# An mLSTM layer with an MLP on one core: one of two large constant products at the start replaced by 80 small ones

## The chip, the cores and the metric

The kernel runs on one core of a Trainium2 chip. Its time is the device time of one execution in microseconds (us). Of the kernel before there are three timed runs, 430.77 us in the median (430.69 to 431.53), and one execution with the hardware profiler on.

## The reference, cut to what matters

The first half is a recurrence over 768 time steps with a 40x40 state for each of 4 batches and 8 heads (mLSTM); the second half is a two-layer MLP on its output.

```python
for t in range(S):                                       # B, H, S, D = 4, 8, 768, 40
    m_new = np.maximum(f_gate[:, :, t] + m, i_gate[:, :, t])
    f_stab = np.exp(f_gate[:, :, t] + m - m_new); i_stab = np.exp(i_gate[:, :, t] - m_new); m = m_new
    C = f_stab * C + i_stab * outer(v_t, k_t)            # 40x40 per batch and head
    n = f_stab * n + i_stab * k_t
    y_t = sigmoid(o_gate_t) * (C @ q_t) / max(|n @ q_t|, 1)
x = y.transpose(0, 2, 1, 3).reshape(3072, 320)
h = x @ w_in                                             # 320 -> 2048
return (h * sigmoid(h)) @ w_out                          # 2048 -> 320
```

Nothing of the reference is touched by the change: the products that it replaces are of a constant with itself, and what they write is never read.

## The kernel before, in words

The 768 time steps are cut into chunks of 64 (`L`), and two batches are taken together, so that there are 24 units (`Unit`). Three units make one step of the MLP (`Step`, eight of them, 384 tokens each), and while step j's MLP runs, the three units of step j+1 are worked into it. The MLP of a step has 16 slices of the 2048 hidden features; of each, `mm1` (L849) makes the hidden values and `mm2` (L901) adds their share of the output. From the second step on each float32 product is split into three of a faster 32-bit kind.

The first three units have nothing to hide behind: they are the head of the program, some 20 us, and they are written out by hand from L987 on. No scheduler moves anything. Each engine runs its instructions in the order in which the code records them, and an instruction waits only for what it reads or overwrites.

The steps of the head that matter here, in the order of TensorE's (PE's) own queue:

- L998 to L1001: `dummy`, a PSUM tile that nobody reads, receives the product of the identity matrix with itself, 128x128 times 128x512 in float32, twice. Each shows as two records of a matmul in the trace. They wait only for `ident`, which GpSimd makes.
- `mask` (L396): for three units a 128x128 by 128x512 product in bfloat16 puts the causal mask into a PSUM tile. It reads `identb` and `maskb`, the bfloat16 copies that ScalarE makes in L117 and L118.
- `scores` (L549): k times q of the first unit, 16 products that show as 32 records. It waits for the DMA of `qk`.
- `small(32)` (L985): 32 more products into `dummy`, 128x128 by 128x64 in bfloat16.
- `expo` (L405, L409): the decay exponents of the first unit. These read `terms`, the gate values split into bfloat16 parts, which VectorE makes in a row of small operations (L167 to L162, called through `gates` and `thirds`) after the two gate tensors have landed.

After that ScalarE takes the exponential (L419), VectorE weighs the scores with it (L576), and so on through three units to the first MLP step at L849.

Of the kernel before, what the change touches and what calls it, by code (L numbers as in the profile page):

```python
# [43 lines left out]
def mlstm_mlp_kernel(  # L44
# [12 lines left out]
    nc = tc.nc  # L57
# [19 lines left out]
    ident = cp.tile([128, 128], F32, name="ident")  # L77
# [9 lines left out]
    identb = cp.tile([128, 128], BF16, name="identb")  # L87
# [76 lines left out]
    def gates(lo, hi):  # L164

        init = NEG if lo == 0 else m_t[:, lo - 1 : lo]
        nc.vector.tensor_tensor_scan(  # L167
            m_t[:, lo:hi], f_t[:, lo:hi], i_t[:, lo:hi], init, op0=ALU.add, op1=ALU.max
        )
        yield  # L170
        l1 = max(lo, 1)
        tt = nc.vector.tensor_tensor
        tt(out=f_t[:, l1:hi], in0=f_t[:, l1:hi], in1=m_t[:, l1 - 1 : hi - 1], op=ALU.add)
        yield
        tt(out=f_t[:, l1:hi], in0=f_t[:, l1:hi], in1=m_t[:, l1:hi], op=ALU.subtract)
        nc.vector.tensor_scalar(f_t[:, l1:hi], f_t[:, l1:hi], -120.0, None, op0=ALU.max)
        if lo == 0:
            nc.vector.memset(f_t[:, 0:1], 0.0)
        yield
        nc.vector.tensor_tensor_scan(  # L180
            LF[:, lo:hi], pat[:, lo:hi], f_t[:, lo:hi], 0.0, op0=ALU.mult, op1=ALU.add
        )
        yield
        tt(out=i_t[:, lo:hi], in0=i_t[:, lo:hi], in1=m_t[:, lo:hi], op=ALU.subtract)
        tt(out=i_t[:, lo:hi], in0=i_t[:, lo:hi], in1=LF[:, lo:hi], op=ALU.subtract)
        yield
# [165 lines left out]
    def wload(n):  # L352
        for p in parts[nload[0] : nload[0] + n]:
            p.load()
        nload[0] = min(nload[0] + n, len(parts))
# [613 lines left out]
    dummy = psO.tile([128, 512], F32, tag="o", name="dummy")  # L969
# [25 lines left out]
    wload(2)  # L995
    u2.load_ko()
    wload(2)
    for _ in range(2):  # L998
        nc.tensor.matmul(  # L999
            dummy, ident, ident.unsqueeze(1).broadcast_to([128, 4, 128]), start=True, stop=True  # L1000
        )  # L1001
    two = gates(2 * L, 4 * L)
    near, far = spread(2 * L, 4 * L, nc.gpsimd), spread_far(4 * L, S, nc.gpsimd)
    late = [gates(4 * L, 8 * L), gates(8 * L, S)]
# [253 lines left out]
```

## Time and profile before

| | us |
|---|---|
| median of three timed runs | 430.77 (430.69 to 431.53) |
| the profiled execution, its whole time | 431.02 |
| its span, first to last instruction | 429.2 |
| PE busy in the span | 422.4 (98%) |
| DVE, ACT, POOL busy | 288.5, 220.6, 124.8 |

PE is TensorE's matmuls and PEld its weight loads, DVE VectorE, ACT ScalarE, POOL GpSimd, SP SyncE, which issues most DMAs. The whole time is 1.82 us longer than the span. A start time in the rows is in us from the start of the span. The profile has a column for the clock that TensorE was granted, as a share of full speed; its record begins only with the first change of the clock, and ahead of that the column reads 1.00. How fast TensorE really went there is read from the pace of its instructions.

### The profile page before, as it was taken

The numbers are of one execution on the slowest core, as the hardware profiler recorded it, in microseconds if no ns is written. First come the engines' busy times: TensorE is split into PE (matmuls) and PEld (weight loads), VectorE is DVE, ScalarE is ACT, GpSimd is POOL, SyncE is SP. The second block draws the span as 40 slices with busy tenths as digits, with TensorE's granted clock in tenths as the row PEclk, the third lists the DMA queues.
The fourth block names the chain that finished last, engine by engine and source line by source line (L and its number), as shares of the span: only waits on it lengthen the run. The fifth ranks groups of instructions, "written<-read, shape, count | busy, mean of one in ns | idle before, by whom it ended". The sixth has DMA issues, their size and how long they took to land.

```text
span 429.2 us, 12518 instructions
## 1 busy us (share of the span) xinstructions
PE 422.4 (98%) x5062; PEld 391.7 (91%) x5062; DVE 288.5 (67%) x650; ACT 220.6 (51%) x481; POOL 124.8 (29%) x135
## 2 busy tenths in 40 slices
PE   8999999999999999999999999999999999999995
PEld 4767677899999999999999999999999999999995
DVE  5888799877887677467765677566764756443342
ACT  7684866755755454454454644444454543353331
POOL 5734135234234423043412344034320400000000
PEclk9999999999999999999999999999999999999999
DMA  8999696334551775127660575316750231001001
GB/s 272 387 366 311 177 299 165 117 89 141 159 169 21 196 196 155 31 61 189 174 172 2 123 218 139 118 25 179 209 163 22 54 94 20 18 9 39 2 2 46
DMA packets 62650, 57.17 MB, mean 133 GB/s; under 512 B 31440, under 2 KB 49184, under 8 KB 62592
## 3 DMA queue, kind: packets, MB, share of 16 engines
q1 hardware_dynamic: 62288, 55.94, 45.7%
q8 instruction: 40, 0.66, 0.7%
q10 hardware_dynamic: 208, 0.26, 0.2%
q0 software_dynamic: 96, 0.16, 0.1%
q14 instruction: 18, 0.15, 0.1%
HBM read 48.99 MB, written 7.36 MB: 131 GB/s over the span
## 4 chain that ended last, share of the span: by engine, by line
PE 80%; issue 17%; DVE 1%; ACT 1%; POOL 0%; POOLq 0%; ACTq 0%; DVEq 0%
PE ph L849 35%; PE pout L901 33%; PE p L549 3%; PE p L637 2%; PE p L620 2%; PE dummy L999 1%; PE pu_u L705 1%; PE pu_h L705 1%; DVE D L576 0%; PE e L396 0%; PE px L794 0%; PE pu L717 0%; PE po L604 0%; PE p L794 0%; POOL qt L533 0%
## 5 line engine op out<-in xcount | busy, mean ns | idle before, releaser
L856 ACT ACTIVATE th<-ph 128x384 f32<-128x384 f32 x128 | 62.4, 488 | 106.7 <-PE ph L849 106.2
L849 PE MATMUL ph<-xh,wh 128*128 128x384 f32 x336 | 113.8, 339 | 0.0
L849 PE MATMUL ph<-xl,wh 128*128 128x384 f32 x336 | 113.6, 338 | 0.0
L901 PE MATMUL pout<-woh,gh 128*128 128x320 f32 x336 | 105.5, 314 | 0.0
L901 PE MATMUL pout<-woh,gl 128*128 128x320 f32 x336 | 103.9, 309 | 0.0
L901 PE MATMUL pout<-wol,gh 128*128 128x320 f32 x336 | 103.3, 307 | 0.0
L876 ACT CAST gh<-th 128x384 fp32r<-128x384 f32 x112 | 57.5, 513 | 81.3 <-DVE th L871 69.9
L880 DVE TENSOR_TENSOR gl<-th,gh 128x384 fp32r<-128x384 f32 x112 | 64.6, 577 | 47.5 <-ACT gh L876 47.5
L871 DVE SCALAR_TENSOR_TENSOR th<-th,ph 128x384 f32<-128x384 f32 x112 | 61.4, 548 | 51.1 <-ACT th L856 50.6
L849 PE MATMUL ph<-xh,wl 128*128 128x384 f32 x224 | 75.9, 339 | 0.0
L747 POOL TENSOR_TENSOR Cm<-Cm,lq 40x328 f32<-40x328 f32 x40 | 30.6, 764 | 114.6 <-PE p L637 111.8
L901 PEld LDWEIGHTS pout<-woh,gh 128*128 128x128 f32 x336 | 63.0, 188 | 0.9
L849 PEld LDWEIGHTS ph<-xh,wh 128*128 128x128 f32 x336 | 63.1, 188 | 0.2
L849 PEld LDWEIGHTS ph<-xl,wh 128*128 128x128 f32 x336 | 63.0, 188 | 0.2
L901 PEld LDWEIGHTS pout<-woh,gl 128*128 128x128 f32 x336 | 63.0, 188 | 0.1
L901 PEld LDWEIGHTS pout<-wol,gh 128*128 128x128 f32 x336 | 63.1, 188 | 0.0
L533 POOL TENSOR_TENSOR qt<-qk,lq 104x512 f32<-104x512 f32 x22 | 29.7, 1348 | 99.4 <-ACT lq L529 89.3
L849 PEld LDWEIGHTS ph<-xh,wl 128*128 128x128 f32 x224 | 42.1, 188 | 0.0
L901 PE MATMUL pout<-wo,g 128*128 128x320 f32 x96 | 28.7, 435 | 0.0
L516 POOL TENSOR_TENSOR D<-D,am 128x512 f32<-128x512 f32 x20 | 26.1, 1303 | 4.0 <-DMA D<-LFd 2.5
L508 POOL TENSOR_TENSOR am<-mask,aT 128x512 f32<-128x512 f32 x20 | 24.1, 1205 | 6.6 <-DVE aT L207 5.1
L576 DVE TENSOR_TENSOR D<-p,D 128x512 f32<-128x512 f32 x24 | 16.5, 689 | 13.7 <-PE p L637 12.3
(136 smaller groups left out, 524.4 us busy)
## 6 DMA issues: line engine op xcount, KB each, us to landing
qk<-in_qk_dram SPq DMA_DIRECT2D x24, 512.0 KB, 5.1
ko<-in_ko_dram SPq DMA_DIRECT2D x24, 320.0 KB, 5.3
wro<-in_w_out_dram SPq DMA_DIRECT2D x8, 640.0 KB, 7.3
D<-LFd SPq DMA_DIRECT2D x40, 128.0 KB, 3.1
lq<-LFd SPq DMA_DIRECT2D x40, 128.0 KB, 4.9
wri<-in_w_in_dram SPq DMA_DIRECT2D x8, 512.0 KB, 6.0
vb<-in_vp_dram SPq DMA_DIRECT2D x48, 82.0 KB, 5.1
out_dram<-ob SPq DMA_DIRECT2D x45, 80.0 KB, 2.1
```

The lines of the kernel that those rows point to most:

```text
L508: nc.gpsimd.tensor_tensor(out=self.am, in0=mask.unsqueeze(1).broadcast_to([128, H, L]), in1=aT[:, self.c, self.p, :].unsqueeze(2).broadcas ...
L516: nc.gpsimd.tensor_tensor(out=self.Dm, in0=self.Dm, in1=self.am, op=ALU.add)
L533: nc.gpsimd.tensor_tensor(out=self.qt, in0=self.q[:KS], in1=self.lq[:KS], op=ALU.mult)
L549: nc.tensor.matmul(self.ps[d * L : (d + 1) * L, a * 4 + j, :], self.k[r, d * 4 + j, :], self.q[r, d * 4 + j, :], start=True, stop=True,)
L576: nc.vector.tensor_tensor(out=self.Dm, in0=self.ps, in1=self.Dm, op=ALU.mult)
L747: nc.gpsimd.tensor_tensor(out=v, in0=v, in1=self.lq[r, :, L - 1].unsqueeze(2).broadcast_to([D, H, D1]), op=ALU.mult,)
L849: nc.tensor.matmul(ph, w, x, start=(i == 0), stop=(i == len(ops) - 1))
L856: nc.scalar.activation(th, ph, AF.Tanh, scale=0.5)
L871: nc.vector.scalar_tensor_tensor(out=th, in0=th, scalar=1.0, in1=ph, op0=ALU.add, op1=ALU.mult)
L876: nc.scalar.copy(gh, th)
L880: nc.vector.tensor_tensor(out=gl, in0=th, in1=gh.bitcast(F32), op=ALU.subtract)
L901: nc.tensor.matmul(self.po[t], g[:, ts], w, start=(fc == 0 and i == 0), stop=(last and i == len(ops) - 1),)
```

## The change: what it does

The second of the two large float32 products is gone. In its place stand 80 products in bfloat16 with a contraction of 128, 32 columns of the constant `identb` as weights and 16 columns of it streamed past, into the corner `dummy[:32, :16]` of the same tile. Each has a weight load of its own, so that PE's queue has 160 rows more. Nothing else in the program is touched.

```diff
-    for _ in range(2):
-        nc.tensor.matmul(
-            dummy, ident, ident.unsqueeze(1).broadcast_to([128, 4, 128]), start=True, stop=True
-        )
+    nc.tensor.matmul(
+        dummy, ident, ident.unsqueeze(1).broadcast_to([128, 4, 128]), start=True, stop=True
+    )
+    for _ in range(80):
+        nc.tensor.matmul(dummy[:32, :16], identb[:, :32], identb[:, :16], start=True, stop=True)
```

At the start of PE's queue this stood before (`e_195`, `e_197` and `e_199` are the PSUM tiles of the three units' exponents, and what an instruction waits for stands in brackets):

```order
L999 MATMUL dummy<-ident 128x512 [waits Pool_49]
L999 MATMUL dummy<-ident 128x512
L396 LDWEIGHTS identb [waits Activation_49]
L396 MATMUL e_195<-maskb,identb 128x512 [waits Activation_49]
L396 LDWEIGHTS identb
L396 MATMUL e_197<-maskb,identb 128x512
L396 LDWEIGHTS identb
L396 MATMUL e_199<-maskb,identb 128x512
L549 MATMUL p_201<-qk_152 64x64 [waits DMAHW2_49]
```

And this stands there now; the lines left out are 79 more pairs of the two rows ahead of them:

```order
L998 MATMUL dummy<-ident 128x512 [waits Pool_49]
L1002 LDWEIGHTS identb [waits Activation_49]
L1002 MATMUL dummy<-identb 32x16
...
L396 LDWEIGHTS identb
L396 MATMUL e_274<-maskb,identb 128x512 [waits Activation_49]
L396 LDWEIGHTS identb
L396 MATMUL e_276<-maskb,identb 128x512
L396 LDWEIGHTS identb
L396 MATMUL e_278<-maskb,identb 128x512
L549 MATMUL p_280<-qk_152 64x64 [waits DMAHW2_49]
```

The wait for ScalarE's `identb` has moved from the first mask product to the first of the small products. On every other engine the order is what it was.

Further down PE's queue, at the end of `small(32)`, the rows are the same before and after but for the numbers of the tiles; this is before:

```order
L985 MATMUL dummy<-maskb,identb 128x64
L405 LDWEIGHTS home [waits DVE_49,Activation_49]
L405 MATMUL e_195<-terms,home 128x64 [waits Activation_49]
L405 LDWEIGHTS home
L405 MATMUL e_195<-terms,home 128x64
```

Here PE waits for VectorE and ScalarE, and all that the change adds stands ahead of this wait.

## Rows read from the trace of the kernel before

**Rows 1.** What PE waited for: engine, tile, line; us in total, times, longest.

```profile
PE dummy L999 <- POOL ident masks.py:199: 1.4, 1, 1.4
PE po L604 <- DVE po L655: 0.4, 1, 0.4
PE p L549 <- DVE D L576: 0.2, 1, 0.2
```

**Rows 2.** Three stretches: length, PE busy (instructions), granted clock, DMA.

```profile
14.90:30.00 15.10, 15.10 (x163) 1.00 1.05 390
30.00:100.00 70.00, 69.96 (x784) 1.00 0.68 200
100.00:424.00 324.00, 323.73 (x3887) 1.00 0.38 100
```

**Rows 3.** Chain that ended last, its start: start us, us, what.

```profile
1.36 3.78 PE dummy L999 x4
5.14 1.20 PE e L396 x3
6.34 0.62 PE p L549 x32
6.97 1.04 PE dummy L985 x32
8.01 0.06 issue
8.06 0.39 PE e L405 x8
8.46 0.36 PE e L409 x2
8.81 0.02 issue
8.83 0.60 ACT D L419
```

**Rows 4.** Timeline of PE and PEld: start us, us, instruction, [idle before].

```profile
3.23 0.33 PEld L999 LDWEIGHTS dummy<-ident 128*128 128x128 f32 x1 [0.52 <-issue]
4.08 1.06 PE L999 MATMUL dummy<-ident 128*128 128x512 f32 x1
4.08 0.15 PEld L396 LDWEIGHTS <-identb 128*128 128x128 bf16 x1 [0.52 <-ACT sel L124]
4.93 0.63 PE L396 MATMUL e<-maskb,identb 128*128 128x512 bf16 x1
5.36 0.15 PEld L396 LDWEIGHTS <-identb 128*128 128x128 bf16 x1 [0.28 <-issue]
5.79 0.55 PE L396 MATMUL e<-maskb,identb 128*128 128x512 bf16 x1
6.27 0.69 PE L549 MATMUL p<-qk 40*64 40x64 f32 x32
6.90 1.11 PE L985 MATMUL dummy<-maskb,identb 128*128 128x64 bf16 x32
7.81 0.19 PE L985 MATMUL dummy<-maskb,identb 128*128 128x64 bf16 x1
```

**Rows 5.** Timeline of ACT, DVE and PEld: what PE waits for.

```profile
2.84 0.30 ACT L117 CAST identb<-ident 128x128 bf16<-128x128 f32 x1
7.50 0.40 ACT L161 COPY terms<-middle 32x256 bf16<-32x256 bf16 x1 [0.58 <-DVE middle L160]
7.50 0.42 DVE L162 TENSOR_TENSOR terms<-rest,middle 32x256 bf16<-32x256 f32 x1
8.03 0.16 PEld L405 LDWEIGHTS <-home 96*128 96x128 bf16 x3
```

**Rows 6.** Durations by line: ns min/median/max, first and last start us.

```profile
L396 PE MATMUL e<-maskb,identb x4: 390/592/631, 4.9 to 16.9; 128*128 128x512 bf16 x4
L985 PEld LDWEIGHTS <-identb x32: 95/98/98, 6.9 to 7.8; 128*128 128x128 bf16 x32
L409 PEld LDWEIGHTS <-terms x2: 106/106/106, 8.4 to 8.4; 96*64 96x64 bf16 x2
```

**Rows 7.** Timeline of PE, a later line with small products.

```profile
18.25 0.44 PE L438 MATMUL eq<-terms,sel 96*64 96x64 bf16 x16
```

## The prediction

> **What bounds the kernel now.** I read the waits of TensorE (PE) first, then its busy time by stretches, then the chain of waits from its start, then the timeline of the first 8 us. The waits show that in 429.2 us PE stands idle for only three things: 1.4 us until `ident` is there, then 0.2 and 0.4 us in the head [rows 1]. The stretches show that from 14.9 us on PE is busy all the time: 15.10 of 15.10 us, 69.96 of 70, 323.73 of 324 [rows 2]. So whatever comes later in the head comes off nowhere behind it: a delay of PE at 15 us is a delay of the end, one to one. The reader can see from this that only the first 15 us matter, and there the chain runs through PE: the large products L999, the masks L396, the scores L549, the 32 fillers L985, and then the exponents L405 and L409, ACT's exponential and so on [rows 3].
>
> At one place on this chain another engine is nearly level with PE. L405 reads `terms`; ACT ends its part at 7.90 and DVE at 7.92 (7.50 plus 0.40 and 0.42), and L405's weight load starts at 8.03, 0.11 later [rows 5]. PE had started its last filler at 7.81 [rows 4]. The fillers come every 0.029 us ((7.81 - 6.90) / 31 [rows 4]), so PE could have gone on at 7.84. It had at most 8.03 - 7.84 = 0.19 us to spare; the chain, which puts this place on PE's account until 8.01 [rows 3], says almost none. I take 0.1. A PE that comes earlier than now thus gains nothing, since L405 waits for DVE; a PE that comes later by D costs about D - 0.1.
>
> The second thing to see is the clock. The granted clock reads 1.00 in the stretches [rows 2], but ahead of 6 us the pace tells another level. The masks stream 512 columns each and start at 4.93, 5.36 and 5.79 [rows 4], one in 0.43 us, which is 1.2 columns per ns, the lower level (1.2 GHz). The same line takes 631 ns at most and 390 ns at 16.9 us [rows 6]; the third one, at 5.79, took 0.55 us [rows 4], a third of the way from the slow duration to the fast one. So two thirds of it (0.28 us) passed at the lower level, and the clock rose to 2.4 GHz at about 6.1 us. Up to then PE had worked without a gap since 1.36.
>
> **The change part by part.** Removed are the third and fourth record of L999. The third one's weights load at 3.23, the fourth record starts at 4.08 and the first mask at 4.93 [rows 4], so the two hold PE from 3.23 to 4.93, 1.70 us at the lower clock.
>
> Added are 80 pairs of a weight load and a product. The first load now waits for `identb`, which ACT finishes at 2.84 + 0.30 = 3.14 [rows 5], just ahead of 3.23: this wait costs nothing by itself, but the load, 0.15 us at the lower clock [rows 4], cannot start much ahead of it, so that the first small product starts at about 3.35. Behind it in PE's queue wait the masks, the scores, the fillers and L405; nobody else waits for `dummy`.
>
> What a pair costs is not in this trace, and it decides the result. From above: the fillers, 128 weight columns and 64 streamed ones, take 29 ns at the full clock; if a small pair were no cheaper, it would take 59 ns at the lower one, 80 of them 4.7 us. From below: L438 starts 16 products of 64 columns within 0.44 - 0.20 = 0.24 us [rows 7] (0.20 is about what one filler takes, 0.19 [rows 4]), 16 ns each at the full clock, because two strips of columns work side by side; if pairs came as fast as that whatever the clock, 80 would take 1.3 us. The nearest row is L438 by strip: two products every 32 ns, so 32 ns for a load of 64 columns and a product of 64 columns in one strip. The small pair loads 32 and streams 16, all in one strip; at half the load it would take 16 ns at the full clock and 32 ns at the lower. I take 32 ns: 80 x 32 = 2.56 us, and the small products end at 3.35 + 2.56 = 5.91 where the large one ended at 4.93.
>
> The Trainium skill, "TensorE: Matmul & The Clock Gate", section "LDWEIGHTS (loading the stationary operand)", has a load cost its columns divided by 1.2 per ns. That is 27 ns for 32 columns, an estimate from that page; 80 of them would be 2.1 us, the delay worked out below 0.2 us and the time 431.0. The trace does not bear the rule out in durations (64 columns 106 ns, 128 columns 95 to 98 ns [rows 6]), and no row here has a load of 32 columns.
>
> Now the rest up to L405, with the clock rising at 6.1 as before. The first mask starts at 5.91, does 0.19 / 0.43 = 44% by 6.1 and the rest at 0.21 us per mask, ending at 6.22; the two others at full clock end at 6.64. Before, the third ended at 6.1 plus a third of 0.21, so 6.14, and L549 started 0.13 later at 6.27 [rows 4]; now it starts at 6.77, 0.50 later. The scores and fillers run at the full clock as before, so PE reaches L405 0.50 late and, with 0.1 to spare, L405 starts 0.4 late. The saving on the masks (0.43 to 0.21) gives back half of what the small products cost; without it the delay were 0.98.
>
> Sum: 0.4 us. Nothing behind it absorbs this: ACT's exponential, DVE's weighing and PE's next products follow each other on the chain. The profiled execution took 431.02 with a span of 429.2, so it would be 431.4; it stands 0.25 above the median of the runs, 430.77. Against the median that is 431.2. By the bounds of a pair, the masks would end at 6.0 (no delay, L405 waits for DVE) at 16 ns; at 59 ns, with 47 pairs done at 6.1 and 33 at 29 ns, the small products end at 7.07, the masks at 7.71, L549 starts 1.57 late, and L405 1.5 late: 432.2.
>
> **The rivals.** *PE still arrives before DVE.* If a pair takes 25 ns or less, the small products end by 5.35 and the masks by 6.2, and L405 goes with DVE as now: 430.8. For it speaks that L438 shows 16 ns; against it that this is at the full clock and over two strips.
>
> *The clock rises later.* Its place is L396, L549 and L985, its price half of their work at the full clock. In the trace the rise came behind 4.7 us of unbroken large streams (1.36 to 6.1). After the change the stretch from 3.35 to 5.91 holds short ones, each streaming 16 columns, that is 13 ns at the pace of the masks, out of 32. If these don't raise the clock as the large product did, PE goes on at the lower level. Price: should the rise come as long after 5.91 as it came after 1.36, at about 10.7, everything up to L405 is slow: masks 1.28, scores 2 x 0.5, fillers 2 x 0.94, gaps 0.2, so L405 starts at about 10.3 instead of 8.03, and L405 and L409 themselves add 0.2: 2.5 us, 433.3. Should it come as soon after 5.91 as it came after the first mask at 4.93, 1.2 us later at 7.1, only the masks are slow: L549 starts at 7.32, 1.0 late, 431.7. In the middle 1.7 us, 432.5. It decides from the point where the rise falls behind about 7.0. For it speaks that only large streams preceded the rise in this trace; against it that PE's queue has no gap either way.
>
> The Trainium skill, same page, section "Part 1: The HAM clock gate", says that the lower level is the default and that activity releases it; the slow masks at the start and the fast one at 16.9 us agree [rows 6]. Whether the small products release it no row here shows.
>
> *Faster by more than the measurement tells.* There would have to be 0.86 us to win (0.2% of 430.77, about what a measurement of this kernel can tell from no change). L405 waits for DVE at 8.03, so PE can win nothing there, and behind 15 us there is no gap to close. That leaves the scatter of the runs, which spans 0.84 us.
>
> **How the numbers follow.** Forecast (clock rises as before, pairs of 25 to 40 ns, delay 0.1 to 0.8): 0.40, 431.2. PE before DVE, no change: 0.15. Pairs much dearer, delay over 0.86: 0.05. Clock later: 0.36, nearly all of it beyond 0.86. Faster: 0.04. So faster 0.04, within 0.2% 0.40 + 0.15 = 0.55, slower 0.05 + 0.36 = 0.41. The range goes from 430.4, the case without delay with some scatter, to 432.8, which takes in the later clock up to 2.0 us; what is left out is its longer end and the faster case. The forecast's own range, with signs of both kinds in play, is 430.6 to 431.6.
>
> **What would show it.** In the profile after: the first L1002 at about 3.35 and the first mask at about 5.9 give the price of a pair; the three masks' durations and the granted clock's record give the rise; L405's start against DVE's L162 gives the delay, and the span should be longer by that and no more. I am wrong if masks and scores are slow throughout (the second rival), if L405 still starts at 8.03 (the first), or if the span moves by something that L405's start doesn't.

## The result

The changed kernel took 433.64 us in the median of 11 runs (433.10 to 436.46). The kernel before, timed beside it, took 431.53 in 11 runs (430.69 to 433.19). The ratio is 1.0059, with a 95% interval of 1.0040 to 1.0078: the change makes the kernel some 2.5 us slower by the ratio, 2.1 us by the medians. My forecast of 431.2 was too low, and the time lies above the stated range (430.4 to 432.8). Part of the miss is the base: the three runs known beforehand lay at the fast end of what the kernel before does. Two single runs of later experiments, of 833.84 and 1058.43 us, stand in no ratio and no median.

| | before | after |
|---|---|---|
| median, us | 431.53 (11 runs) | 433.64 (11 runs) |
| profiled execution / span, us | 431.02 / 429.2 | 433.16 / 431.4 |
| first exponent product L405 starts, us | 8.06 | 9.76 |
| clock rises to 2.4 GHz (its record begins), us | 6.1 | 10.2 |

The timeline of PE in the profile after, from its start (start us, us, instruction), stands against [rows 4]:

```profile
1.36 2.08 PE L998 MATMUL dummy<-ident 128*128 128x512 f32 x2 [1.36 <-POOL ident masks.py:199]
3.37 2.30 PE L1002 MATMUL dummy<-identb 128*32 128x16 bf16 x80
5.61 1.46 PE L396 MATMUL e<-maskb,identb 128*128 128x512 bf16 x3
7.00 1.13 PE L549 MATMUL p<-qk 40*64 40x64 f32 x32
8.06 1.89 PE L985 MATMUL dummy<-maskb,identb 128*128 128x64 bf16 x32
9.76 0.62 PE L405 MATMUL e<-terms,home 96*128 96x64 bf16 x8
10.31 0.41 PE L409 MATMUL e<-sel,terms 96*64 96x512 bf16 x2
10.65 0.41 PE L405 MATMUL e<-terms,home 96*128 96x64 bf16 x8
```

The reader is to see two things. The small products cost a little less than was forecast: they start at 3.37 and the masks at 5.61, 80 pairs at 28 ns where I had taken 32. Then everything is slow. The masks come 0.46 us apart ((7.00 - 5.61) / 3), the scores take 1.06 us up to the fillers where they took 0.63 (6.27 to 6.90 in [rows 4]), the fillers 1.70 up to L405. The first group of L405 takes 0.62 us and the second, behind 10.2 us, 0.41. Up to there PE is at the lower level, 1.2 GHz, though it never stood idle since 1.36.

The chain of waits after, against [rows 3]: it runs through the same lines, and no longer comes near DVE's `terms` at 7.92.

```profile
1.36 2.08 PE dummy L998 x2
3.44 2.23 PE dummy L1002 x80
5.67 1.39 PE e L396 x3
7.07 1.06 PE p L549 x32
8.13 1.82 PE dummy L985 x32
9.95 0.43 PE e L405 x8
```

What PE waited for after, against [rows 1], and its stretches, against [rows 2]:

```profile
PE dummy L998 <- POOL ident masks.py:199: 1.4, 1, 1.4
PE pu L717 <- issue: 0.4, 1, 0.4
PE p L637 <- POOL qt L533: 0.3, 1, 0.3
PE p L549 <- DVE D L576: 0.2, 1, 0.2
```

```profile
14.90:30.00 15.10, 14.70 (x186) 1.00 1.04 387
30.00:100.00 70.00, 69.69 (x796) 1.00 0.66 189
100.00:426.00 326.00, 325.74 (x3900) 1.00 0.38 102
```

Of the 2.2 us in the span, 1.70 are there when L405 starts (9.76 against 8.06), and that first group adds 0.2 (0.55 us up to L409 against 0.32). The wait of 0.4 us in L717 is new; its releaser "issue" means that the profile shows nothing that PE waited for. The wait of L604 for DVE, as long, [rows 1] is gone for it. New too is the wait of 0.3 us for POOL, in the stretch from 30 us on (69.69 of 70.00 us against 69.96 [rows 2]).

### The profile page after: what moved, and what is told of

Same layout as the page of the kernel before. It is cut to its first block, busy times and chain, and to the rows that moved or that the text cites. A ratio compares the mean times of both kernels' runs of the same rounds, so it can differ in the third digit from the quotient of the medians.

```text
span 431.4 us, 12674 instructions
## 1 busy us (share of the span) xinstructions
PE 424.4 (98%) x5140; PEld 394.4 (91%) x5140; DVE 289.4 (67%) x650; ACT 220.6 (51%) x481; POOL 125.5 (29%) x135
## 4 chain that ended last, share of the span: by engine, by line
PE 76%; issue 17%; DVE 2%; ACT 2%; DMA 1%; POOL 1%; POOLq 0%; ACTq 0%; DVEq 0%
PE ph L849 32%; PE pout L901 31%; PE p L549 3%; PE p L637 2%; PE p L620 2%; DMA wro<-in_w_out_dram 1%; PE pu_u L705 1%; POOL qt L533 1%; PE pu L717 1%; PE dummy L1002 1%; PE pu_h L705 0%; PE dummy L998 0%; PE po L604 0%; PE dummy L985 0%; PE e L396 0%
```

## The experiments

The theories, as the expectations name them: A, the small products do not let the clock rise as the large one did (A1: for their narrow weights, A2: for their short stream). B, it is the time that PE spends in them. C, the place of the rise is chance. D, small products make what follows them slow whatever stood ahead. E, it is the 160 rows added to PE's queue. Ratios are against the kernel before in the same rounds. The place of the clock's rise is the start of its record in a profile.

**Large products in the same time.**

```diff
-    for _ in range(80):
-        nc.tensor.matmul(dummy[:32, :16], identb[:, :32], identb[:, :16], start=True, stop=True)
+    warm(5)                       # 5 products in bfloat16, 128x128 by 128x512
```

> The 80 small products are replaced by 5 large bfloat16 ones (128 weight columns, 512 streamed) that hold PE about as long, 5 x 0.43 = 2.1 us against 2.2. Theory A (short products do not raise the clock as large ones do): the rise is back ahead of 7 us, L405 starts at 8.0 to 8.5, and the time is 431 to 432, 2 us less than the changed kernel's 433.6. Theory B (it is the time that PE spends there, 0.5 us more than before, and the cover lost): the time stays at 433 to 434. Theory C: as often late as the changed kernel.

Measured: ratio 1.0006 (0.9990 to 1.0022). The timeline of PE:

```profile
3.33 2.15 PE L981 MATMUL dummy<-maskb,identb 128*128 128x512 bf16 x5
5.32 0.81 PE L396 MATMUL e<-maskb,identb 128*128 128x512 bf16 x3
6.06 0.69 PE L549 MATMUL p<-qk 40*64 40x64 f32 x32
8.06 0.31 PE L405 MATMUL e<-terms,home 96*128 96x64 bf16 x5 [0.26 <-DVE terms L162]
```

The clock rose at 5.2 us. PE comes to the masks at about the same time as in the changed kernel (5.32 against 5.61) and runs them fast; it even waits 0.26 us for DVE. The profiled execution (430.38) was the fastest of 12, but the ratio takes them all. Theory B falls: the time that PE spends there is not what costs.

**Nothing in its place.** The loop of 80 is left out.

> One large float32 product and nothing in the place of the second. PE comes to the masks at about 3.3 us and to L549 at 5.2, when its data is there. Theory A: how late the clock rises decides; if as late as in the changed kernel (10.2 us), masks, scores and fillers all run at the lower clock, but they start some 2 us earlier, so L405 starts at about 8.2 and the work behind it is slow until the rise: 431.5 to 432.5. If the small products had only cost time and not clock (theory B), the clock rises by 6 to 7 and the time is 430.7 to 431.2.

Measured: ratio 1.0034 (1.0016 to 1.0053), and a median of 433.39 against 431.50, above what either theory had expected. In the first profile (430.97, the fastest of 12 runs) the clock rose at 5.5 us and L405 began at 8.06. A second profile:

> One large product and nothing else, a second look. Its times fall into two groups, 431 to 433 and 433.9 to 434.4; the first look (430.97) had the rise at 5.5 us and L405 at 8.03. Theory A: the slower group has the rise behind 8 us, L405 still close to 8.1 to 8.5 since PE comes early, and slow work behind it. If the rise is ahead of 8 us in a slow execution, its time is lost elsewhere (a fall of the clock, a stall inside a group).

It took 434.06, and its clock rose only at 17.4 us; L405 started at 8.08, as PE came early, and the head behind it was slow:

```profile
8.08 0.58 PE L405 MATMUL e<-terms,home 96*128 96x64 bf16 x8
11.80 1.13 PE L549 MATMUL p<-qk 40*64 40x64 f32 x32
15.22 1.32 PE L717 MATMUL pu<-vb,kw 128*40 128x82 f32 x16
16.32 1.82 PE L604 MATMUL po<-vb,D 128*64 128x82 f32 x32
```

With an early clock the kernel thus did without the second large product (430.97); with a late one it lost 3 us (434.06). So that product mattered here by the clock, and the 80 small ones did not stand in for it: with them the ratio was 1.0059 (1.0040 to 1.0078), without anything 1.0034. These two intervals overlap, so which of the two is the slower kernel is open.

**The kernel before and after again.**

> The kernel before, unchanged, for one more look at where its clock rises. Theory A (the clock follows what PE did before): the rise lies again ahead of the exponents L405, between 5 and 7.5 us, and L405 starts within 0.5 us of 8.03. Theory C (the place of the rise is a matter of chance from execution to execution, and the one trace of the changed kernel drew a late one): the rise may lie anywhere, 10 us too.

> The kernel before, a third look. Theory A: the rise lies at 4.5 to 7.5 us and L405 starts at 8.0 to 8.3; whether the clock falls again behind 11 us, as in one of two looks, is open: 430.7 without, 432 to 434 with a fall.

> The changed kernel once more, for a look at where its clock rises. Theory A (the small products do not raise the clock as the large one did): the rise lies again behind 8 us, masks and scores run at the lower clock and L405 starts at 9 us or later. Theory C (chance from execution to execution): the rise may lie ahead of 6 us, and L405 then starts at 8.0 to 8.4.

> The changed kernel, timed on the same chip in the same rounds as the one with 32 streamed columns, and a third look at it. Theory A: rise behind 8 us, L405 at 9.5 to 9.8 as in the two looks so far, 433 to 434 in the median and 2 us over the kernel before.

Measured: in the two further profiles before, the clock rose at 4.6 and 5.0 us and L405 began at 8.06 both times; in the two further profiles after, it rose at 11.2 and 10.2, and L405 began at 9.76 both times. L405 in these four, two before and two after:

```profile
8.06 0.39 PE L405 MATMUL e<-terms,home 96*128 96x64 bf16 x8 [0.83 <-DVE terms L162]
8.06 0.39 PE L405 MATMUL e<-terms,home 96*128 96x64 bf16 x8 [0.63 <-DVE terms L162]
9.76 0.61 PE L405 MATMUL e<-terms,home 96*128 96x64 bf16 x8
9.76 0.61 PE L405 MATMUL e<-terms,home 96*128 96x64 bf16 x8
```

Timed again, the changed kernel had 433.32 against 431.73 and a ratio of 1.0053 (1.0032 to 1.0074). Chance moves the rise within each kernel, but the two kernels do not overlap in three profiles each, so theory C falls as an explanation of the difference. It explains part of the scatter. In the first of the further profiles before (433.89) the clock rose early and fell again; three stretches, with PE's busy time, the granted clock and the DMA share:

```profile
4.60:11.40 6.80, 5.17 (x119) 1.00 0.97 291
11.40:18.20 6.80, 6.80 (x136) 0.50 0.92 324
18.20:30.00 11.80, 11.80 (x111) 1.00 1.04 393
```

Here 0.50 is the lower level. Between the rise and the fall PE had waited 0.8 us for DVE and 0.8 us for a DMA.

**Which part of the small product.** The weights 128 columns wide, the stream still 16:

```diff
-        nc.tensor.matmul(dummy[:32, :16], identb[:, :32], identb[:, :16], start=True, stop=True)
+        nc.tensor.matmul(dummy[:, :16], identb, identb[:, :16], start=True, stop=True)
```

> 80 products with 128 weight columns in place of 32, and still 16 streamed columns each. Theory A in the form that the narrow weights are what the clock misses: the rise is back ahead of 7 us and the time at 431 to 432. Theory A in the form that it is the short stream: the rise stays at about 10 us and the time at 433 to 434. Theory B: as the changed kernel if a pair takes as long, about 28 ns.

Measured: ratio 1.0036 (1.0014 to 1.0058), and the clock rose at 11.6 us:

```profile
3.23 2.33 PE L1002 MATMUL dummy<-identb 128*128 128x16 bf16 x80
5.41 1.44 PE L396 MATMUL e<-maskb,identb 128*128 128x512 bf16 x3
9.54 0.61 PE L405 MATMUL e<-terms,home 96*128 96x64 bf16 x8
```

The weights still 32 columns wide, but 512 streamed, and five of them:

```diff
-    for _ in range(80):
-        nc.tensor.matmul(dummy[:32, :16], identb[:, :32], identb[:, :16], start=True, stop=True)
+    for _ in range(5):
+        nc.tensor.matmul(
+            dummy[:32], identb[:, :32], maskb.unsqueeze(1).broadcast_to([128, 8, L]), start=True, stop=True
+        )
```

> The 80 small products are replaced by 5 that load the same 32 weight columns and stream 512 columns each: PE's time there as with the small ones (5 x 0.43 = 2.1 us), but only 10 rows in PE's queue in place of 160. It tells the clock's part from the part of the added instructions (PE stood still inside a group of products at 17 to 19 us in every kernel with the 160 rows, 0.4 to 1.1 us, with nothing to wait for). Theory A1 (narrow products do not raise the clock, and that is most of the loss): rise behind 8 us, L405 at 9 or later, 432.5 to 433.5. Theory A2 (it is the short stream): rise ahead of 7 us, L405 at 8.0 to 8.4, 431.5 to 432. Theory E (the added instructions are most of the loss): 431.5 to 432 whatever the clock does. In A and E alike there is no stall of over 0.3 us inside a group at 17 to 19 us.

Measured: ratio 1.0004 (0.9989 to 1.0018), and the clock rose at 4.9 us:

```profile
3.37 2.00 PE L1002 MATMUL dummy<-maskb,identb 128*32 128x512 bf16 x5
5.30 0.82 PE L396 MATMUL e<-maskb,identb 128*128 128x512 bf16 x3
8.06 0.31 PE L405 MATMUL e<-terms,home 96*128 96x64 bf16 x5 [0.28 <-DVE terms L162]
```

Wide weights with the short stream leave the clock down, narrow weights with the long stream do not (one profile each; the ratios go the same way). A1 falls. But this kernel has 10 rows where the changed one has 160, so A2 and E are not yet told apart.

**The stream alone, with all 160 rows.**

```diff
-        nc.tensor.matmul(dummy[:32, :16], identb[:, :32], identb[:, :16], start=True, stop=True)
+        nc.tensor.matmul(dummy[:32, :32], identb[:, :32], identb[:, :32], start=True, stop=True)
```

> One number of the change: the 80 products stream 32 columns each in place of 16. A pair took 28 ns with 16 columns at the lower clock, and 32 columns are 27 ns there, so PE's time and the 160 added rows stay what they are. Theory A2 (the short stream keeps the clock down, and that is most of the loss): the clock rises at 5 to 8 us, L405 starts at 8.1 to 8.8, and the time is 1.2 to 2 us under the changed kernel's. Theory E (the 160 rows, by the stalls of PE's instruction stream, are most of it): the time stays within 0.5 us of the changed kernel's, 433 to 434, whatever the clock does. If the clock stays down here too: rise behind 9 us, as the changed kernel.

> A second look at 32 streamed columns, since the place of the rise differs from execution to execution: theory A2 has it at 5 to 8 us again and L405 at 8.1 to 8.8; theory E leaves it open, but has a stall of 0.4 to 1.1 us inside a group of products at 17 to 19 us, as in the changed kernel.

Measured: ratio 1.0026 (1.0008 to 1.0043), beside 1.0053 for the changed kernel in the same rounds. The clock rose at 6.6 us in both profiles. The first one's timeline:

```profile
3.36 2.32 PE L1002 MATMUL dummy<-identb 128*32 128x32 bf16 x80
5.61 1.27 PE L396 MATMUL e<-maskb,identb 128*128 128x512 bf16 x3
6.82 0.70 PE L549 MATMUL p<-qk 40*64 40x64 f32 x32
7.44 1.11 PE L985 MATMUL dummy<-maskb,identb 128*128 128x64 bf16 x32
8.39 0.40 PE L405 MATMUL e<-terms,home 96*128 96x64 bf16 x8
```

Up to 5.61 us this row by row is the changed kernel. Then the masks end sooner, scores and fillers are fast, and L405 starts 0.33 us later than before instead of 1.70. One number, 16 to 32, thus gives back 1.37 us at L405 (L405 starts at 8.38 in the second profile). That streaming 16 columns in place of 32 brought the late clock and the late L405 is shown, by two profiles against three. Why it does, no run tells. In the time it gives back about 1.2 us by the ratios (0.0027 of 431.7) and 0.9 by the medians (432.42 against 433.32). The two intervals overlap, so that this is the larger part of the loss in time is likely and not shown. What is left, 0.0026 or 1.1 us (0.7 by the medians), is more than the 0.33 at L405.

**All 80, behind both large products.** The loop of 80 is put into the kernel before, behind its two products.

> Both large float32 products as before, and the 80 small ones behind them: what is added to the kernel before is the small products' time alone. Theory A: the clock rises at 5 to 7.5 us as before, the small products start at about 4.95 and take 1.1 to 2.2 us (14 to 28 ns each), the masks come that much later but at the full clock, and L405 starts 0.8 to 1.8 us late: 432 to 433 against 431.5 in the median. Theory D (the small products make what follows them slow too, whatever stood ahead of them): the rise is behind 9 us and the time 433.5 or more.

Measured: ratio 1.0048 (1.0018 to 1.0077), and a median of 433.24 against 431.71. The clock rose at 4.3 us and stayed up, which speaks against D:

```profile
4.71 2.16 PE L1003 MATMUL dummy<-identb 128*32 128x16 bf16 x80
6.80 0.82 PE L396 MATMUL e<-maskb,identb 128*128 128x512 bf16 x3
9.12 0.34 PE L405 MATMUL e<-terms,home 96*128 96x64 bf16 x6
```

The small products start at 4.71 and the masks at 6.80, 26 ns for a pair at the higher level where 28 ns were taken at the lower; L405 starts at 9.12, 1.06 late. The loss is 2 us by the ratio and 1.5 us by the medians: two of the 12 runs, 437.79 and 438.56, have a mean granted clock of 0.992 where the others have 0.997 to 1.000, so that the clock was longer at the lower level there. In the profile (432.62, against 431.02 in the first one before) PE stands still once more, in a place that theory E points to:

```profile
PE pu L717 <- issue: 1.0, 1, 1.0
```

The same pause, inside a group of 16 equal products with nothing to wait for, stands in the profiles after (0.4 us in the first, 1.1 in the second, none in the third), in the second profile with 32 columns (0.9) and in the one with wide weights (0.7). In the second profile after:

```profile
17.83 0.69 PE L717 MATMUL pu<-vb,kw 128*40 128x82 f32 x13
19.63 0.34 PE L717 MATMUL pu<-vb,kw 128*40 128x82 f32 x3 [1.10 <-issue]
```

Its DMA queues from 17.3 to 18.4 us (packets, MB, share of 16 engines):

```profile
q1 hardware_dynamic: 190, 0.40, 96.3%
q8 instruction: 1, 0.02, 5.5%
```

One packet of the queue whose kind is "instruction" lies there, among data that keep the DMA engines full. It ends at 18.35 us, and PE goes on at 19.63, 1.28 later. In the other profiles with this pause PE goes on 1.2 to 1.5 us behind such a packet too. That PE waited for its next instructions fits; no run took that packet away.

But the kernel before has such a pause as well, without the 160 rows. In its first and third profile DVE's rows are the same to 0.01 us, and the same product goes on at 14.42 in the one and at 15.02 in the other:

```profile
14.42 0.79 PE L604 MATMUL po<-vb,D 128*64 128x82 f32 x16 [0.44 <-DVE po L655]
15.02 0.79 PE L604 MATMUL po<-vb,D 128*64 128x82 f32 x16 [1.04 <-DVE den L660]
```

So the last 0.6 us of the second wait are not DVE's, though the row names it; PE goes on there 1.49 us behind an instruction packet. From the start of L405 to the end of the span it is 421.1 and 421.8 us in these two, 421.6, 422.4 and 420.8 after, 421.8 and 422.0 with 32 columns, and 421.7 here. The profiles thus show no cost of the 160 rows behind L405; one of some tenths would be lost in this scatter.

**Three tries at a faster kernel**, none of which beat the kernel before. Fewer rows (five large products as in the first experiment, and the 32 fillers replaced by four large ones):

```diff
-    small(32)
+    warm(4)
```

> A try at a faster kernel: 5 large bfloat16 products in place of the second float32 one, and 4 large ones (512 columns) in place of the 32 fillers of 64 columns, so that PE's queue has 46 rows less ahead of the exponents than before. If the stalls inside groups follow the number of PE's instructions (theory E), the stall at 13 to 15 us of the kernel before (0.4 us) goes or shrinks: 430.3 to 431.3 in the median against 431.6. If only the clock counts: as with the 5 large products alone, 431.5 to 432.2.

Measured: 1.0052 (1.0030 to 1.0074), and a median of 434.22, above what either reading had expected. The clock rose at 4.4 us, but a pause now fell into the products behind the third unit's values, where the kernel before has none:

```profile
15.91 0.50 PE L604 MATMUL po<-Cm,qt 104*64 104x82 f32 x8 [0.91 <-issue]
```

So the pauses do not shrink with the number of rows, and theory E in that form falls. They keep their place in PE's own queue: counted in records of products, each with a weight load, the pause stands behind 220 here, behind 221 in the third profile before, and behind 347 in the five profiles with the 160 rows that have it. From 220 to 347 are 127 products, or 254 rows. Which work of the head the pause falls into thus follows from the number of rows ahead.

A good part of this kernel's loss has another source: five of its 12 runs (434.66 to 436.41) have a mean granted clock of 0.992 to 0.994, where none of the 23 runs before in the same rounds is below 0.997. In these five the clock was at the lower level for longer than in the others. The other seven have a median of 432.84.

An earlier start (nine products of a tile of ones that DVE writes first, in place of the two of `ident`; PE starts at 0.99 us), and the same with extra products in two waits of the head:

```diff
+    onesb = cp.tile([128, L], BF16, name="onesb")
+    nc.vector.memset(onesb, 1.0)
...
+    for _ in range(9):
+        nc.tensor.matmul(dummy, onesb[:, :1].broadcast_to([128, 128]), onesb.unsqueeze(1).broadcast_to([128, H, L]), start=True, stop=True)
...
+    small(8)                      # second kernel only, ahead of u2.scores()
...
+    for _ in range(3):            # second kernel only, behind u2.place()
+        nc.tensor.matmul(
+            u2.po, identb, maskb[:, :D1].unsqueeze(1).broadcast_to([128, H, D1]), start=True, stop=True
+        )
```

> A try at a faster kernel: the two float32 products are replaced by nine bfloat16 ones of 128 weight columns and 512 streamed, on a tile of ones that DVE writes as its first instruction, so that PE starts at about 0.9 us instead of 1.36 and streams without a gap until the masks. Theory A: the clock rises at 4 to 7 us and never behind L405, so the slow executions of the kernel before get rarer: median 430.7 to 431.3 against 431.5. Theory C: no different from before, 431.5 and the same scatter.

> As the kernel with the early start, and in the two places of the head where PE waits for DVE (ahead of the third unit's scores and of its values) it gets products that nobody reads, 8 of 128x64 and 3 of 128x328, 0.2 and 0.4 us at the full clock. In one look at the kernel before the clock had risen at 4.6 us and fallen again from 11.4 to 18.2. If it is these waits that let it fall, the fall goes, and with it the slowest executions: median 430.6 to 431.1, highest below 432. If the products only delay PE: 0.2 to 0.5 us slower than the kernel with the early start.

Measured: 1.0028 (1.0007 to 1.0049) and 1.0011 (0.9988 to 1.0034), with medians of 432.98 and 432.04 against 431.71; neither came to the time hoped for. The first exponent product starts at 8.06 in both, as DVE lets it; pauses with the releaser "issue" (0.30 and 0.45 us, both in the products that are L604 in the kernel before) are there too, and the first kernel has two more (0.4 and 0.2). The second one's extra products do not keep the clock from falling: two of its 12 runs, 434.90 and 434.92, have a mean granted clock of 0.992 where the others have 0.997 to 1.000.

## Why the prediction was wrong

- *Only the first 15 us matter*: right in the main. Of the 2.2 us in the span 1.70 were there at L405, and behind 15 us PE stood still for only 0.7 us in that profile (14.70 of 15.10 us and 69.69 of 70.00).
- *The price of a pair, 32 ns*: it was 28 ns at the lower level. The Trainium skill, "TensorE: Matmul & The Clock Gate", "LDWEIGHTS (loading the stationary operand)", had given 27 ns, an estimate from its rule of columns divided by 1.2 per ns. The number agrees, the rule does not: with 128 weight columns a pair took 27 ns too ((5.41 - 3.23) / 80, the kernel with wide weights), where the rule would give 107, an estimate. The same page, in "Wait — 56ns, not 53.3ns?", has starts never closer than about 25 ns however short the product; the 26 ns at the higher level agree, while L438, over two strips, starts a product every 16 ns on the average [rows 7]. I had expected a pair to take half as long at the higher level; in the sum that made little.
- *With the clock rising at 6.1 as before*: this is the step that failed. In the changed kernel the rise came at 10.2 to 11.2 us, masks, scores and fillers ran at the lower level, and L405 was 1.70 late where I had worked out 0.4. With an earlier rise the sum came near: with the clock at 6.6 us (32 streamed columns) L549 was 0.55 late, forecast 0.50, and L405 0.33. That is in part luck, as the later rise, the cheaper pair and a spare time before DVE of 0.22 in place of 0.1 nearly cancel.
- *The rival with the late clock*, chance 0.36: this is what happened, by its longer end. For a rise at 10.7 I had L405 at 10.3 and a loss of 2.5 us; with the rise at 10.2 L405 came at 9.76, 0.5 sooner, as the small products ended 0.30 sooner and the fillers took 1.70 us in place of 1.88. That my middle price of 1.7 us is the delay at L405 is luck: it was meant for a rise between 7.1 and 10.7. The stated range left this longer end out. I gave the rival the smaller chance because PE's queue had no gap; the runs show that an unbroken queue of these products was not enough here.
- *The rival with PE ahead of DVE* had a slip: with pairs of 25 ns the masks end at 6.37 by the working of the sum, and not at 6.2, so it needed pairs of some 22 ns. At the 28 ns measured it did not come to bear.
- *The delay at L405 is the whole loss*: wrong by the first group at the lower clock (0.2 us), which I had put into the rival and not into the forecast. What is left beyond that is 0.2 us by the medians and 0.6 by the ratio, and it stays open. With 32 columns 1.1 us are lost for 0.33 at L405, and with both large products 2 us for 1.06; by the medians it is 0.7 and 1.5. I had priced neither pauses of PE nor a clock that falls again. The profiles show both, with the 160 rows and without them, and they do not show that the rows bring more of either.
- *The base*: I took 430.77; over 11 runs it was 431.53. The scatter that I read as noise has causes that a profile shows: a clock that falls again, and pauses that differ.

## What to carry to other kernels

A product that is there to bring the clock up must be judged by where the paces of the products behind it change, not by whether it keeps PE's queue full. Where a sum assumes that the clock stays as it was, the case in which it does not is worth its own price from rows at the lower level; here the price of its longer end, 2.5 us, was near the loss, and the chance and the range were too small. And a pause of an engine that waits for nothing is worth counting in rows of its queue: here it kept its count, and changes to the work ahead only changed what it fell into.

## What the runs showed that was not expected

The clock rises and falls at different places in executions of one kernel: before, it rose at 4.6, 5.0 and 6.1 us, and once it fell from 11.4 to 18.2 us, while the program is the same. With one large product alone the rise came at 5.5 us in one execution and at 17.4 in another. A pair of a 32-column load and a 16-column product takes 28 ns at 1.2 GHz and 26 ns at 2.4 GHz, so the clock hardly matters to it. And PE paused for up to 1.1 us inside a group of products that wait for nothing, behind the same number of products in its queue each time: 220 or 221 in kernels without the 160 rows, 347 in those with them.
